# Storing the last chunk of a fused attention and gated-FFN kernel tile by tile, each tile copied out of PSUM by two engines in halves

## The chip, the cores and the metric

The kernel runs on 1 core of one Trainium2 chip. The metric is the device time of one launch in microseconds (us); lower is better. Beside it the hardware profiler gives one profiled launch of each kernel, whose span (first to last instruction) is some 2 us shorter than the time of a launch.

## The reference

Two stages. The first is attention over channels (B = 4, N = 6016 rows, C = 256 channels), the second a gated feed-forward network over the 24,064 rows that come out.

```python
def _attn_ref(q, k, v, tau):
    qn = q / (np.linalg.norm(q, axis=1, keepdims=True) + 1e-06)
    kn = k / (np.linalg.norm(k, axis=1, keepdims=True) + 1e-06)
    s = kn.transpose(0, 2, 1) @ qn / tau
    s = s - s.max(-1, keepdims=True)
    a = np.exp(s)
    a /= a.sum(-1, keepdims=True) + 1e-09
    return (v @ a).astype(np.float32)

def _moe_ref(x, w_gate, w_val, w_out):
    gate = 1.0 / (1.0 + np.exp(-(x @ w_gate)))
    val = x @ w_val
    return (gate * val @ w_out).astype(np.float32)
```

The inputs are fp32 random numbers, the output is fp32 of shape 24064 x 256.

## The kernel before

The rows of a batch are worked in 12 chunks: 11 of four 128-row tiles and a last one of three, since 6016/128 = 47. For each chunk the kernel computes gate and value products (`glu`) and, one chunk later, the output product of the chunk before (`out_mms`). An output tile of 128 x 256 fp32 collects in PSUM (the memory in which matmuls add up) over 12 matmuls, is copied to SBUF (from which the transfer takes it), and when the chunk's last tile is there, one transfer stores all of them.

```python
def out_mms(b, ci, n0, n1):
    t0, nt = groups[ci]
    hT = hts[b, ci]
    for n in range(n0, min(n1, nt * FC)):
        s, f = divmod(n, FC)
        if n == 0:
            ffn[b, ci] = opool.tile([P, TPC, C], FP32, tag="osb", name="out_sb")
        if f == 0:
            ffn["ps"] = pso.tile([P, C], FP32, tag="o", name="ps_o")
        mm(ffn["ps"], hT[:, f, ds(s * P, P)], w_out_sb[:, f, :], f == 0, f == FC - 1)
        if f == FC - 1:
            pending.append((ffn[b, ci], s, ffn["ps"], b, ci))

def flush():
    while pending:
        out_sb, s, ps, b, ci = pending.pop(0)
        t0, nt = groups[ci]
        nc.vector.tensor_copy(out=out_sb[:, s, :], in_=ps)
        if s == nt - 1:
            nc.sync.dma_start(out=out_rows[b][:, t0 : t0 + nt, :], in_=out_sb[:, :nt, :])

# ... the main loop; after it, the last chunk has only its output product left:
for s in range(groups[NCH - 1][1]):
    out_mms(*prev, s * FC, (s + 1) * FC)
    flush()
```

The framework in which it is written gives every transfer that SyncE or ScalarE issues one of eight completion semaphores (counters that tell when a transfer has landed), in turn, and puts closing waits for all of them at the end of SyncE's program.

Of the kernel before, what the change touches and what calls it, by code (L numbers as in the profile page):

```python
# [17 lines left out]
def kernel(  # L18
# [20 lines left out]
    nc = tc.nc  # L39
# [5 lines left out]
    B, N, C = q.shape  # L45
# [9 lines left out]
    NCH = (NT + TPC - 1) // TPC  # L55
# [8 lines left out]
    out_rows = out.rearrange("(b p t) c -> b p t c", b=B, p=P)  # L64
# [45 lines left out]
    t0, nt = groups0[0]  # L110
# [24 lines left out]
    for fg in range(NFG):  # L135
        for w, src in enumerate((moe_w_gate, moe_w_val)):
            nc.gpsimd.dma_start(
                out=w_sb[w][fg],
                in_=src.rearrange("(t p) f -> p t f", p=P)[:, :, ds(fg * FG, FG)],
# [290 lines left out]
    def flush():  # L430
        while pending:
            out_sb, s, ps, b, ci = pending.pop(0)
            t0, nt = groups[ci]
            nc.vector.tensor_copy(out=out_sb[:, s, :], in_=ps)  # L434
            if s == nt - 1:
                nc.sync.dma_start(out=out_rows[b][:, t0 : t0 + nt, :], in_=out_sb[:, :nt, :])


    def busy(n):
# [101 lines left out]
    for b in range(B):  # L541
        side = side_work(b)
        for ci in range(NCH):
            block = b + 1 < B and ci in (9, 10)
            for f in range(FC):
                glu(b, ci, f)
                flush()
                if prev is not None and not block:
                    out_mms(*prev, f * TPC, (f + 1) * TPC)
                for fn, a in side.get((ci, f), ()):  # L550
                    fn(*a)
                if (b, ci) == (0, 0) and f < len(gh_order) - 5:
                    gh(0, 5 + f, pso, "o")
            if prev is not None and block:
                for s in range(TPC):
                    for fn, a in side.get((ci, FC + s), ()):
                        fn(*a)
                    out_mms(*prev, s * FC, (s + 1) * FC)
                    flush()
            prev = (b, ci)  # L560
# [3 lines that stand above are left out]
# [35 lines left out]
```

## Time and profile before

| | before |
|---|---|
| time, median of 6 launches (3 of them taken before the change was run) | 832.36 us (832.06 to 832.71) |
| span of the profiled launch | 830.4 us |
| TensorE busy | 99% of the span |
| start of the last sigmoid (`g_sb`) | 822.03 us |
| from there to the end of the span, the **tail** | 8.39 us |

The last sigmoid serves as a mark: nothing before it is touched by the change, and everything that is touched lies after it. The tail is taken from the records at full resolution (the span ends at 830.415), so it may differ by 0.01 from what the rounded lines give. The lines of this profile stand in the prediction below.

### The profile page before, as it was taken

To read this page: it belongs to the slowest core of one execution; us is meant where nothing else is said; L and a number is where in the kernel's file an instruction comes from. 1 tells how busy PE (TensorE), PEld (TensorE's weight loads), DVE (VectorE), ACT (ScalarE), POOL (GpSimd) and SP (SyncE) were. 2 spreads that over 40 slices of the span, in tenths; PEclk is the share of its full clock that TensorE was granted. 3 is DMA by queue.
4 is the path that set the end of the run, shared out by engine and by line. 5 is a ranking of instruction groups with operands and counts; after the bars stand their busy time and mean duration, and the time that the engine had idled before them with its cause. 6 is when DMAs were issued, how large, how long until landed. Compare 5 with 4: busy or idle time off the path is not lost.

```text
span 830.4 us, 14273 instructions
## 1 busy us (share of the span) xinstructions
PE 818.9 (99%) x5463; PEld 513.8 (62%) x5474; DVE 570.4 (69%) x981; ACT 390.8 (47%) x642; POOL 82.9 (10%) x159
## 2 busy tenths in 40 slices
PE   8899999999999999999999999999999999999998
PEld 7656666666666666665576666666566566666666
DVE  2477777777667777777767777777766666666664
ACT  4554444445644444444654444444555444444442
POOL 5532100002110100000220020000000000000000
PEclk9999999999999999999999999999999999999999
DMA  9999623236755543233974453223222324323211
GB/s 209 207 206 189 130 52 88 51 63 123 141 105 105 102 105 60 56 52 79 161 140 97 84 112 77 51 75 66 62 56 65 75 51 82 71 49 69 47 36 71
DMA packets 78740, 77.21 MB, mean 93 GB/s; under 512 B 50768, under 2 KB 55632, under 8 KB 78672
## 3 DMA queue, kind: packets, MB, share of 16 engines
q0 software_dynamic: 23920, 38.81, 28.2%
q1 hardware_dynamic: 54608, 36.97, 17.4%
q8 instruction: 43, 0.70, 0.3%
q10 hardware_dynamic: 144, 0.52, 0.2%
q14 instruction: 25, 0.20, 0.1%
HBM read 78.64 MB, written 24.64 MB: 124 GB/s over the span
## 4 chain that ended last, share of the span: by engine, by line
PE 95%; DMA 3%; DVE 1%; issue 0%; POOL 0%; ACT 0%; POOLq 0%; DVEq 0%; ACTq 0%
PE ps_o L88 30%; PE ps_gate L88 29%; PE ps_val L88 29%; PE ps_s L88 4%; DMA k_sb<-in_k_dram 3%; PE ps_gh L88 2%; PE ps_n L88 0%; DVE gh_G L363 0%; PE ps_busy L88 0%; POOL q_sb L97 0%; PE ps_r L88 0%; DVE hT L408 0%; PE ps_rk L88 0%; DVE gh_H L363 0%; DVE x_sb L293 0%
## 5 line engine op out<-in xcount | busy, mean ns | idle before, releaser
L408 DVE TENSOR_TENSOR hT<-ps_val,g_sb 128x512 bf16<-128x512 f32 (+1 forms) x576 | 391.4, 680 | 214.7 <-ACT g_sb L407 209.5
L407 ACT ACTIVATE g_sb<-ps_gate 128x512 bf16<-128x512 f32 (+1 forms) x576 | 338.2, 588 | 386.6 <-PE ps_gate L88 379.0
L88 PE MATMUL ps_gate<-vT,gh_G 128*128 128x512 bf16 (+1 forms) x1152 | 337.6, 375 | 0.6 <-ACT g_sb L407 0.4
L88 PE MATMUL ps_val<-vT,gh_H 128*128 128x512 bf16 (+1 forms) x1152 | 337.7, 375 | 0.2
L88 PE MATMUL ps_o<-w_out_sb,hT 128*128 128x256 bf16 x2256 | 326.2, 273 | 0.0
L88 PEld LDWEIGHTS <-hT 128*128 128x128 bf16 x2256 | 220.7, 98 | 124.7
L88 PEld LDWEIGHTS <-gh_H 128*128 128x128 bf16 x1152 | 112.7, 98 | 131.5 <-DVE gh_H L363 0.5
L88 PEld LDWEIGHTS <-gh_G 128*128 128x128 bf16 x1152 | 112.5, 98 | 37.9 <-issue 0.6
L106 POOL DMA_DIRECT2D v_sb<-in_v_dram x48 | 25.6, 533 | 625.6 <-DMA vT<-v_sb 517.4
L434 DVE COPY out_sb<-ps_o 128x256 f32<-128x256 f32 x188 | 77.8, 414 | 13.5 <-PE ps_o L88 13.5
L88 PE MATMUL ps_s<-k_sb,q_sb 128*128 128x256 bf16 x376 | 66.8, 275 | 4.9 <-DMA k_sb<-in_k_dram 3.2
L212 DVE TENSOR_TENSOR acc<-acc,sq 128x1024 bf16<-128x1024 bf16 (+1 forms) x66 | 44.2, 670 | 0.0
L88 PEld LDWEIGHTS <-q_sb 128*128 128x128 bf16 x376 | 36.8, 98 | 11.1 <-issue 4.5
L173 DVE TENSOR_TENSOR sq<-q_sb 128x1024 bf16<-128x1024 bf16 (+2 forms) x45 | 30.0, 669 | 18.5 <-DMA q_sb<-in_q_dram 10.7
L97 POOL DMA_DIRECT2D q_sb<-in_q_dram x48 | 26.3, 548 | 15.6 <-DMA q_sb<-in_q_dram 7.9
L97 POOL DMA_DIRECT2D k_sb<-in_k_dram x48 | 26.4, 550 | 12.0 <-ACT g_sb L407 5.4
L173 DVE TENSOR_TENSOR sq<-k_sb 128x1024 bf16<-128x1024 bf16 (+2 forms) x34 | 22.4, 658 | 1.1 <-PE ps_n L88 1.1
L361 ACT ACTIVATE gh_G<-ps_gh,rrow 128x512 bf16<-128x512 f32 x22 | 15.1, 687 | 12.9 <-PE ps_gh L88 9.1
L171 ACT ACTIVATE sq<-k_sb 128x1024 bf16<-128x1024 bf16 (+1 forms) x12 | 12.1, 1020 | 14.7 <-DMA k_sb<-in_k_dram 13.2
L363 DVE TENSOR_SCALAR gh_H<-ps_gh,rrow 128x512 bf16<-128x512 f32 x23 | 17.1, 743 | 1.6 <-PE ps_gh L88 1.6
L88 PE MATMUL ps_busy<-ones_bf 128*128 128x128 bf16 x182 | 16.6, 244 | 1.1 <-DVE shift L125 1.1
L88 PEld LDWEIGHTS <-ones_bf 128*128 128x128 bf16 x194 | 14.6, 110 | 1.5 <-DVE shift L125 1.1
(54 smaller groups left out, 112.6 us busy)
## 6 DMA issues: line engine op xcount, KB each, us to landing
out_dram<-out_sb SPq DMA_DIRECT2D x44, 512.0 KB, 2.9
v_sb<-in_v_dram POOLq DMA_DIRECT2D x44, 256.0 KB, 3.9
q_sb<-in_q_dram POOLq DMA_DIRECT2D x43, 256.0 KB, 7.1
k_sb<-in_k_dram POOLq DMA_DIRECT2D x43, 256.0 KB, 8.3
out_dram<-out_sb SPq DMA_DIRECT2D x4, 384.0 KB, 2.5
w_gate<-in_moe_w_gate_dram POOLq DMA_DIRECT2D x3, 256.0 KB, 6.8
w_val<-in_moe_w_val_dram POOLq DMA_DIRECT2D x3, 256.0 KB, 6.8
w_out_sb<-in_moe_w_out_dram POOLq DMA_DIRECT2D x1, 768.0 KB, 11.9
```

The source lines that it names most:

```text
L88: nc.tensor.matmul(out, lhsT=lhsT, rhs=rhs, start=start, stop=stop, **kw)
L97: nc.gpsimd.dma_start(out=tl[:, :nt, :], in_=rows(src, b)[:, t0 : t0 + nt, :])
L106: nc.gpsimd.dma_start(out=v_sb[:, :nt, :], in_=rows(v, b)[:, t0 : t0 + nt, :])
L171: nc.scalar.activation(out=sq[:, :nt, :], in_=src[:, :nt, :], func=ACT.Square)
L173: engine.tensor_tensor(out=sq[:, :nt, :], in0=src[:, :nt, :], in1=src[:, :nt, :], op=ALU.mult)
L212: nc.vector.tensor_tensor(out=acc[:, :nt, :], in0=acc[:, :nt, :], in1=st[b]["sq", w][:, :nt, :], op=ALU.add)
L361: nc.scalar.activation(out=dst, in_=ps, func=ACT.Copy, scale=r)
L363: nc.vector.tensor_scalar(out=dst, in0=ps, scalar1=r, scalar2=None, op0=ALU.mult)
L407: nc.scalar.activation(out=g_sb[:, :n], in_=ps_gate[:, :n], func=ACT.Sigmoid)
L408: nc.vector.tensor_tensor(out=hts[b, ci][:, f, :n], in0=ps_val[:, :n], in1=g_sb[:, :n], op=ALU.mult)
L434: nc.vector.tensor_copy(out=out_sb[:, s, :], in_=ps)
```

## The change

The intent is to shorten the end. The last chunk's three tiles go out as they are ready, each in its own store, so that only a third of the bytes is left when the last matmul is over; and each tile's copy is shared by VectorE and ScalarE.

```diff
-            nc.vector.tensor_copy(out=out_sb[:, s, :], in_=ps)
-            if s == nt - 1:
-                nc.sync.dma_start(out=out_rows[b][:, t0 : t0 + nt, :], in_=out_sb[:, :nt, :])
+            if (b, ci) != (B - 1, NCH - 1):
+                nc.vector.tensor_copy(out=out_sb[:, s, :], in_=ps)
+                if s == nt - 1:
+                    nc.sync.dma_start(out=out_rows[b][:, t0 : t0 + nt, :], in_=out_sb[:, :nt, :])
+                continue
+
+            half = C // 2
+            nc.vector.tensor_copy(out=out_sb[:, s, :half], in_=ps[:, :half])
+            nc.scalar.copy(out_sb[:, s, half:], ps[:, half:])
+            nc.sync.dma_start(out=out_rows[b][:, t0 + s, :], in_=out_sb[:, s, :])
```

## The prediction

> **What bounds the kernel now.** I read the page first, then the timeline of the last eight microseconds, then the issues and packets of the last store, then the one place where this kernel already splits a copy between two engines.
>
> ```profile
> span 830.4 us, 14273 instructions
> PE 818.9 (99%) x5463; PEld 513.8 (62%) x5474; DVE 570.4 (69%) x981; ACT 390.8 (47%) x642; POOL 82.9 (10%) x159
> PE 95%; DMA 3%; DVE 1%; issue 0%; POOL 0%; ACT 0%; POOLq 0%; DVEq 0%; ACTq 0%
> L434 DVE COPY out_sb<-ps_o 128x256 f32<-128x256 f32 x188 | 77.8, 414 | 13.5 <-PE ps_o L88 13.5
> ```
>
> TensorE is busy 99% of the span and is 95% of the chain that ended last. The change touches no matmul, so whatever it does must happen after the last matmul, or by delaying one. The row of L434 gives the price of the operation that is cut in two: 414 ns for 128x256 fp32 out of PSUM. Only 3 of these 188 copies, those of the last chunk (3 tiles, because 47 tiles leave a last group of three), are changed. The timeline of the end, start and duration first:
>
> ```profile
> 822.15 4.53 PE L88 MATMUL ps_o<-w_out_sb,hT 128*128 128x256 bf16 x40
> 823.47 4.04 SPq L436 DMA_DIRECT2D out_dram<-out_sb  x2
> 824.10 0.42 DVE L434 COPY out_sb<-ps_o 128x256 f32<-128x256 f32 x1 [0.66 <-PE ps_o L88]
> 825.41 0.42 DVE L434 COPY out_sb<-ps_o 128x256 f32<-128x256 f32 x1 [0.88 <-PE ps_o L88]
> 826.72 0.42 DVE L434 COPY out_sb<-ps_o 128x256 f32<-128x256 f32 x1 [0.89 <-PE ps_o L88]
> ```
>
> The reader is to see that the three output tiles finish 1.31 us apart, that VectorE waits for each of them and that the first two copies have nothing behind them until the third is done: one store takes all three tiles. A timeline of 827.0 to 830.4 alone shows its issue at 827.17, 0.03 us after the last copy. From there to the end of the span are 3.2 us with no compute at all. Looking at DMA in that stretch (40 slices of 0.085 us):
>
> ```profile
> DMA  0200000000047997996999740000000000000000
> DMA packets 146, 0.40 MB, mean 117 GB/s; under 512 B 17, under 2 KB 17, under 8 KB 146
> q1 hardware_dynamic: 146, 0.40, 29.9%
> out_dram<-out_sb SPq DMA_DIRECT2D x1, 384.0 KB, 2.3
> SPq L594 <- DMA out_dram<-out_sb: 1.5, 1, 1.5
> ```
>
> The store needs some 0.8 us before its first packet, about 1.1 us of packets, and has landed 2.3 us after issue, at about 829.5; SyncE waits for that landing, and then the program's closing steps take 0.9 us. So the tail is: copy 0.42, gap 0.03, store 2.3, close 0.9. Only the copy and the packet part of the store can be changed by this diff.
>
> **What the Trainium skill says.** Perfetto Trace Analysis, section "Summary: the profiler window per engine type": the record of such a DMA instruction covers its issue and not the movement of data. The trace agrees: the chain of waits ends with the copy at 827.14 although the span runs to 830.4, so the chain alone would hide the part that the change aims at.
>
> PSUM — Partial Sum Buffer, section "PSUM bank collisions raise a hardware error": two engines may not access one bank on the same partitions at once, two reads included, even at different columns. Both halves of one output tile lie in one bank (256 fp32 a partition), so they must be ordered. The trace shows this ordering where the kernel already splits a copy (two rows of the timeline around 51 us):
>
> ```profile
> 51.42 0.41 DVE L382 COPY vT<-ps_tp 128x512 bf16<-128x512 bf16 x1
> 51.87 0.58 ACT L383 COPY vT<-ps_tp 128x512 bf16<-128x512 bf16 x1 [1.20 <-DVE vT L382]
> ```
>
> ScalarE had been idle for 1.20 us, its half was as ready as the other, and it began only 0.03 us after VectorE's half had ended. In the order of the changed kernel's instructions each new ScalarE copy likewise waits for VectorE, and each new store waits for ScalarE. So "in halves" means one after the other here.
>
> VectorE: DVE Perf Modes, section "The TRN2 errata — SBUF-src ops pay a fixed extra latency per instruction" gives for PSUM to SBUF 120 + N cycles at 0.96 GHz on VectorE and 172 + N at 1.2 GHz on ScalarE. For 256 fp32 on VectorE that is 392 ns against 414 measured, so the form holds: much of a copy is fixed, and half the columns don't take half the time.
>
> DMA: Bandwidth & Descriptors, section "Anatomy of one DMA — SWDGE (gpsimd) path" fits 2.0 us + bytes/436 GB/s. For 384 KB that is 2.9 us; measured are 2.3 on SyncE's queue, so the fixed part is smaller here, near 1.3 to 1.4, but the form (a large fixed part and a part by bytes) is the same.
>
> **The change part by part.** Nothing before the last chunk changes: the instructions of all five engines stand in the same order with the same waits up to there, on the order listing, so 822 us of the time are the same.
>
> *The copies of tiles 1 and 2* (done at 824.5 and 825.8 before) become two halves in a row, some 0.2 us later each, and each is followed by its own store. They lie beside matmuls: the third tile's first matmul (at about 825.4) needs tile 1's PSUM buffer back and now waits for ScalarE, but that half is over by about 824.7. No effect on the end. Their two stores of 128 KB go out at about 824.7 and 826.0; with 0.8 us to the first packet and 0.4 us of packets, the second is through by about 827.2, before the last store's packets, which start at about 828.1. SyncE is busy 0.34 us per issue in 1.31 us. No effect on the end either.
>
> *The last copy.* VectorE, 128 columns: 414 minus 128 columns' worth. In the table by form, the gate multiply takes 691 ns at 512 columns and 556 at 384, 135 per 128. So 414 - 135 = 279 ns. ScalarE, 128 columns: its sigmoid takes 597 ns at 512 and 487 at 384, 110 per 128; from the 585 ns copy above, 585 - 3 x 110 = 255 ns; from a 387 ns activation of 258 columns out of PSUM, 387 - 110 = 277. I take 265. The handover is the 0.035 us seen at 51.87. Together 0.28 + 0.035 + 0.265 = 0.58 against 0.42: **+0.16 us**, on the path.
>
> *The last store.* 128 KB in place of 384. In the stretch shown, queue 1 used 29.9% of 3.4 us, 1.02 us on each of the 16 engines, for 3 KB rows. The same view over 823.4 to 827.0 holds the chunk before with its 4 KB rows: 37.2% of 3.6 us, 1.34 us. So a further KB in each row costs 0.32 us, and an estimate for 1 KB rows is 1.02 - 2 x 0.32 = 0.38 us. The store should land 0.64 us sooner after its issue, 1.65 us instead of 2.3: **-0.64 us**, on the path. As a check, the page's median landings are 2.9 us at 512 KB and 2.5 at 384, 0.4 per 128 KB, which would give 0.8 less; but those medians fall among other traffic, so I keep 0.64.
>
> *Sum:* +0.16 - 0.64 = **-0.48 us**, of 832.23: **831.75 us**, 0.06% faster.
>
> **The rivals.** (a) *The halves run side by side.* Then the copy takes the longer half, 0.28, in place of 0.42, and the sum is -0.14 - 0.64 = -0.78: 831.45 us. Against it speaks the wait of 1.20 us shown above and the listing's waits. (b) *The landing is all fixed cost*, a small store takes as long as a large one, since most of it is the acknowledgement of the write. Then only the slower copy remains: 832.4 us. Against it: the packets take 1.1 of the 2.3 us in the view, and landing follows size in the medians. (c) *The extra stores get in the way*: the last store's packets queue behind tile 2's, or short rows run at a much lower rate than long ones, say at twice the time per byte, 0.7 us instead of 0.38. The gain shrinks to 0.1 or 0.2 us: 832.05. Against it: 0.9 us lie between tile 2's last packet and the last store's first. (d) *TensorE is held* at the third tile by the PSUM buffer that now comes free through ScalarE. That would need the copy to take 1.3 us instead of 0.58.
>
> **Range and chances.** The mechanisms span 831.45 to 832.4. The three times before spread over 832.15 to 832.71, so a median can shift by 0.2 without cause. I give 831.2 to 832.4. The whole tail after the last matmul is under 4 us, 0.5% of the time, so no outcome within it reaches 2% (16.6 us) either way: within 2% 0.99, the rest only for a disturbed run.
>
> **What would show each step right or wrong.** In the changed profile: three 128x128 copies on VectorE of about 0.28 us and three on ScalarE of about 0.265, each ScalarE one starting some 0.03 us after VectorE's end (if they overlap, rival a holds); the last issue about 0.6 us after the last matmul instead of 0.45; a landing of about 1.65 us for the last 128 KB (2.2 would be rival b, 1.9 to 2.0 rival c); a DMA view in which tile 2's packets are over before the last ones start; matmuls ending at the same 826.7; and a span near 829.9. The prediction is wrong if the span is not shorter, if TensorE shows a gap before the third tile, or if the program's close grows.

## The result

| | before | after |
|---|---|---|
| time, median of 6 launches | 832.36 us | 832.38 us |
| lowest to highest | 832.06 to 832.71 | 831.92 to 833.14 |
| span of the profiled launch | 830.4 us | 829.8 us |
| tail | 8.39 us | 8.29 us |

The ratio is 1.0001 with a 95% interval of 0.9988 to 1.0014: the same. Ratios are the mean time of one kernel's fast runs over that of the other's measured beside it, so not quite the ratio of the medians. The six runs of the changed kernel and the profiled run of the kernel before were at granted clocks of 0.998 to 1.0; the six times of the kernel before lie within 0.08% of each other.

The predicted 0.48 us is not there. What makes this worth reading is that the profiled span *is* shorter, by 0.6 us, about as predicted, and that nearly all of this is an accident. First the end of the timeline of the changed kernel (start, duration, engine, line, operation, in brackets the idle time before it and what ended it):

```profile
823.56 0.29 DVE L441 COPY out_sb<-ps_o 128x128 f32<-128x128 f32 x1 [0.66 <-PE ps_o L88]
823.88 0.27 ACT L442 COPY out_sb<-ps_o 128x128 f32<-128x128 f32 x1 [1.91 <-DVE out_sb L441]
824.17 2.95 SPq L443 DMA_DIRECT2D out_dram<-out_sb  x3
824.87 0.29 DVE L441 COPY out_sb<-ps_o 128x128 f32<-128x128 f32 x1 [1.02 <-PE ps_o L88]
825.20 0.27 ACT L442 COPY out_sb<-ps_o 128x128 f32<-128x128 f32 x1 [1.04 <-DVE out_sb L441]
826.18 0.29 DVE L441 COPY out_sb<-ps_o 128x128 f32<-128x128 f32 x1 [1.02 <-PE ps_o L88]
826.50 0.27 ACT L442 COPY out_sb<-ps_o 128x128 f32<-128x128 f32 x1 [1.04 <-DVE out_sb L441]
```

The halves run one after the other, as predicted: each ScalarE copy starts 0.03 us after VectorE's end. But the last copy begins at 826.18, and before it began at 826.72. That is 0.54 us *earlier*, although nothing ahead of it had been changed. The chain that ended last shows where the 0.54 us is from. Its lines (start, duration, link) around 32 us, of the kernel before:

```profile
21.80 10.48 DMA k_sb<-in_k_dram
32.33 1.03 PE ps_s L88 x8
```

and of the changed kernel:

```profile
22.00 9.75 DMA k_sb<-in_k_dram
31.79 1.03 PE ps_s L88 x8
```

The start of the kernel waits for loads of `k`. In this launch the last of these ended 0.54 us sooner, and comparing the matmuls of the two traces one by one, their difference stays at -0.54 us from there to the last matmul. Below, the kernel before run again arrives 0.81 us sooner than itself. So this part belongs to no kernel.

That leaves 0.09 us in the tail (8.387 against 8.293). The last store itself did what it should. The DMA view of the changed kernel from 826.4 to 829.8 (40 slices of 0.085 us):

```profile
DMA  9996200000000029998300000000000000000000
DMA packets 281, 0.25 MB, mean 75 GB/s; under 512 B 33, under 2 KB 281, under 8 KB 281
out_dram<-out_sb SPq DMA_DIRECT2D x1, 128.0 KB, 1.7
```

The first block is the second tile's store, over well before the last tile's store begins to move; that one needs some 0.5 us of packets where 384 KB needed 1.1, and lands 1.7 us after its issue where 2.3 were needed. The gain of 0.6 us on the store was made, the copy cost 0.17 us of it, and 0.37 us were lost after the landing. The view of SyncE's closing line, in the kernel before, first the stretch from 827.5 to 829.4, then from 829.4 to 829.6 (operation, count, shortest/median/longest ns, first and last start):

```profile
L594 SPq EVENT_SEMAPHORE  x8: 28/28/28, 827.5 to 828.0; - x8
...
L594 SPq EVENT_SEMAPHORE  x1: 27/27/27, 829.5 to 829.5; - x1
L594 SPq DRAIN  x1: 13/13/13, 829.6 to 829.6; - x1
```

and in the changed kernel, from 827.13 to 828.45 and from 828.45 to 828.96:

```profile
L601 SPq EVENT_SEMAPHORE  x2: 17/22/28, 827.2 to 827.5; - x2
...
L601 SPq EVENT_SEMAPHORE  x7: 28/28/28, 828.5 to 828.9; - x7
L601 SPq DRAIN  x1: 13/13/13, 828.9 to 828.9; - x1
```

These are nine closing waits, carried out strictly one after the other, at a pace of about 0.062 us. Before, eight of them were passed while the last store was still in flight, and only the ninth stood after the landing at 829.49. Afterwards only two were passed in flight; the third waits for the landing at 828.49, and six more follow it: 6 x 0.062 = 0.37 us. The built programs say why:

```
closing waits of SyncE, in order:   (first)  HW0  HW1  HW2  HW3  HW4  HW5  HW6  HW7
before: the last store signals on                                               HW7
after:  the three stores signal on           HW0  HW1                           HW7
        in the order HW7, HW0, HW1: the last one signals on HW1
```

One store became three, the turn of the eight semaphores moved on by two, and the last store's semaphore came to stand near the front of the row instead of at its end.

### The profile page after: what moved, and what is told of

Read it like the earlier page. It is cut to its first block, busy times and chain, and to the rows that moved or that the text cites. A ratio compares the mean times of both kernels' runs of the same rounds, so it can differ in the third digit from the quotient of the medians.

```text
span 829.8 us, 14281 instructions
## 1 busy us (share of the span) xinstructions
PE 817.7 (99%) x5463; PEld 512.9 (62%) x5474; DVE 569.7 (69%) x981; ACT 391.9 (47%) x645; POOL 83.2 (10%) x159
## 4 chain that ended last, share of the span: by engine, by line
PE 95%; DMA 3%; DVE 0%; issue 0%; POOL 0%; ACT 0%; POOLq 0%; DVEq 0%; ACTq 0%
PE ps_o L88 30%; PE ps_gate L88 29%; PE ps_val L88 29%; PE ps_s L88 4%; DMA k_sb<-in_k_dram 3%; PE ps_gh L88 2%; PE ps_n L88 0%; DVE gh_G L363 0%; PE ps_busy L88 0%; POOL q_sb L97 0%; PE ps_r L88 0%; DVE hT L408 0%; PE ps_rk L88 0%; DVE gh_H L363 0%; DVE x_sb L293 0%
```

## The experiments

The theory: three terms add up in the tail, namely the copy (+0.17 us for halves in a row), the store (-0.63) and the number of closing waits left after the last landing (0.062 us each). Rivals: the longer close comes from having several stores in flight, or from their late landing; or the halves are a gain after all; or the start's 0.54 us belongs to the change. All kernels gave correct results. Kernels looked at once carry the state "unknown", as a single run on one core does, and their times are not compared; what is compared is the tail, whose first part (last sigmoid to last copy) was 4.69 us in all of these profiles but that of the two-bank kernel. A further 0.02 to 0.03 us lie between the copy's end and the store's issue in every one. The terms, in us:

| kernel | last copy | issue to landing | landing to first closing drain | rest of close | tail |
|---|---|---|---|---|---|
| before | 0.42 | 2.32 | 0.08 | 0.84 | 8.39 |
| before, again | 0.42 | 2.31 | 0.08 | 0.84 | 8.38 |
| after | 0.59 | 1.69 | 0.45 | 0.84 | 8.29 |
| after, again | 0.59 | 1.70 | 0.45 | 0.84 | 8.30 |
| three stores, whole copies | 0.42 | 1.69 | 0.45 | 0.84 | 8.12 |
| one store, halves | 0.59 | 2.32 | 0.08 | 0.84 | 8.55 |
| before, one store cut early | 0.42 | 2.31 | 0.51 | 0.84 | 8.81 |
| before, four cut | 0.42 | 2.32 | 0.36 | 0.94 | 8.76 |
| before, five cut | 0.42 | 2.31 | 0.30 | 1.25 | 9.02 |
| after, six cut | 0.59 | 1.70 | 0.09 | 0.84 | 7.94 |
| three stores, whole copies, six cut | 0.42 | 1.70 | 0.08 | 0.84 | 7.77 |
| the same, again | 0.42 | 1.75 | 0.08 | 0.82 | 7.80 |
| two banks, six cut | 0.32 | 1.84 | 0.08 | 0.84 | 7.79 |

### The kernels run again

> The kernel before, unchanged, for the scatter. Theory: the tail repeats at 8.38 within 0.03, while the start of the last sigmoid (822.03 before, 821.49 after) moves by several tenths because the loads of the first 32 us end earlier or later. Rival, that the changed kernel's earlier arrival of 0.54 us belongs to the change: 822.03 again within 0.1.

> The changed kernel, unchanged, for the scatter: tail 8.29 within 0.03; the start of the last sigmoid anywhere from 821.4 to 822.7. Rival: 821.49 again within 0.1.

No edit. The tails repeat within 0.01 us. The last sigmoid of the kernel before started at 821.22, 0.81 us before its own first profile, and the span was 829.6, less than that of the changed kernel; the changed kernel's started at 821.38. So the rival falls: the 0.54 us at the start came with the launch and not with the change. The tails of these pairs agree to 0.01 us (a third pair below to 0.03), while a span is known only to about 1 us.

### Three stores, copies whole

```diff
             half = C // 2
-            nc.vector.tensor_copy(out=out_sb[:, s, :half], in_=ps[:, :half])
-            nc.scalar.copy(out_sb[:, s, half:], ps[:, half:])
+            nc.vector.tensor_copy(out=out_sb[:, s, :], in_=ps)
```

> Tail means: end of the span minus the start of the last sigmoid on ScalarE (before 830.4 - 822.03 = 8.38 us, after 829.8 - 821.49 = 8.29). This kernel keeps the three stores and gives each tile's copy back to VectorE whole. If the two halves run one after the other, as the trace says, the whole copy saves 0.29 + 0.03 + 0.27 - 0.42 = 0.17 us: tail 8.12. If the halves had in truth been a gain (side by side), the tail would be longer than 8.29, near 8.42.

The tail was 8.12 as expected. The second half of the change, two engines on one copy, is a loss of 0.17 us.

### One store, copies in halves

```diff
-            nc.sync.dma_start(out=out_rows[b][:, t0 + s, :], in_=out_sb[:, s, :])
+            if s == nt - 1:
+                nc.sync.dma_start(out=out_rows[b][:, t0 : t0 + nt, :], in_=out_sb[:, :nt, :])
```

> Halves kept, but one store of 384 KB for the whole chunk as before. Theory: only the copy's 0.17 us is added to the tail of before: 8.38 + 0.17 = 8.55, the landing is 2.3 us again and the closing row of waits is passed under the store's flight as before. Rival, that the halves cost nothing: 8.38.

The tail was 8.55, as expected. The same 0.17 us appear from the other side, and with one store the close is short again.

### The last store's place in the row of waits

To move the place and nothing else, stores far ahead of the end are cut in two. Each cut moves the turn of the semaphores on by one. In the kernel before, with one cut (n = 1):

```diff
+            if s == 1 and b == B - 1 and ci < 1:
+                nc.sync.dma_start(out=out_rows[b][:, t0 : t0 + 2, :], in_=out_sb[:, :2, :])
             if s == nt - 1:
-                nc.sync.dma_start(out=out_rows[b][:, t0 : t0 + nt, :], in_=out_sb[:, :nt, :])
+                r0 = 2 if b == B - 1 and ci < 1 else 0
+                nc.sync.dma_start(out=out_rows[b][:, t0 + r0 : t0 + nt, :], in_=out_sb[:, r0:nt, :])
```

> The kernel before with one much earlier store cut in two, so that all later transfers of SyncE and ScalarE use the next of the eight completion semaphores in turn, and the last store signals on the first of the eight that SyncE waits for at the close, not on the last one. The tail's own work is unchanged: one copy, one store of 384 KB. Theory of the position: 7 more waits at 0.062 us stand after the landing, tail 8.38 + 0.43 = 8.81, the closing steps after landing 1.35 us in place of 0.92. Rival, that the longer close comes from the number of stores in flight at the end or from their late landing: tail 8.38 unchanged.

The tail was 8.81, as expected, with the copy and the store unchanged. The same closing line of SyncE in this kernel, from 828.80 to 829.35; the store landed at 828.82:

```profile
L597 SPq EVENT_SEMAPHORE  x8: 27/28/28, 828.8 to 829.3; - x8
L597 SPq DRAIN  x1: 13/13/13, 829.3 to 829.3; - x1
```

The last store's own wait and the seven behind it all stand after the landing. There is one store at the end here and no late small one, so the rivals "several stores in flight" and "late landing" fall: a kernel whose tail does exactly the work of the kernel before became 0.42 us longer in its tail because a store 163 us ahead of the last one had been cut in two.

The counter-test is the same edit with `ci < 6` in the changed kernel, which puts its last store on the last semaphore:

> The changed kernel with six much earlier stores cut in two, so that its last store signals on the last of the eight semaphores of the closing row again. Theory of the position: the six waits after the landing go under the store's flight, 6 x 0.062 = 0.37 us less: tail 8.29 - 0.37 = 7.92, which is 0.46 below before, as the prediction had it (0.48). Rival (number of stores at the end): 8.29 unchanged.

The tail was 7.94 where 7.92 was expected. From 828.85 to 829.02, around the landing at 828.91:

```profile
L604 SPq EVENT_SEMAPHORE  x1: 28/28/28, 828.9 to 828.9; - x1
L604 SPq DRAIN  x1: 13/13/13, 829.0 to 829.0; - x1
```

Only the store's own wait is left after it, none behind that. With the place put right, the change gives 0.45 us, which is what had been predicted for it (0.48).

### Does the cost go by the number of waits?

The kernel before with four cuts (`ci < 4`) and with five (`ci < 5`):

> As the kernel before with four early stores cut in two: the last store signals on the fourth of the eight semaphores, so four waits stand after its landing. Theory of the position, if the cost goes by the number of waits: 4 x 0.062 = 0.25, tail 8.63. If being off the last place costs a fixed amount, it equals the run with one store cut, 8.81; if it is the number of stores, 8.38.

> The kernel before with five early stores cut in two: last store on the fifth of the eight semaphores, three waits after the landing: 3 x 0.062 = 0.19, tail 8.38 + 0.19 = 8.57. The run with four cut stores gave 8.76 where 8.63 was expected; 0.10 of that was one closing step of SyncE of 116 ns in place of 7. If that step belongs to cutting many stores, it shows here too (8.67); if it is an accident, 8.57.

The tails were 8.76 and 9.02 where 8.63 and 8.57 had been expected: missed, both. The term in question behaved: landing to first drain was 0.51, 0.36 and 0.30 us with seven, four and three waits left, against 0.08 with none, within 0.04 of 0.08 + 0.062 n. What missed is another step. SyncE's closing drains in the two kernels (from 828.3 to 829.9, and from 829.2 to the end):

```profile
L597 SPq DRAIN  x3: 7/13/116, 829.0 to 829.6; - x3
...
L597 SPq DRAIN  x3: 7/13/116, 829.6 to 830.3; - x3
```

One drain took 116 ns in place of 7; with four cuts it was the third, with five the second. It also began some 0.3 us late: 0.40 us after the step before it where other kernels have 0.09 us (third drain), and 0.37 us where they have 0.07 (second drain). Every cut puts two more instructions into SyncE's program (the transfer and a wait), and the slow step moved two instructions forward. In the kernels with six cuts and three stores, which have eight instructions more than that with four cuts, a gap of 0.37 to 0.38 us stands eight instructions further forward still, among the closing waits. No landing ended it: none came within 0.15 us ahead of its end, where a wait otherwise ends 0.02 us after the landing. There it lies under the flight of the last store and costs nothing.

So the slow step looks tied to a fixed place in SyncE's program, and the guess that it was an accident was wrong. Counted from the start of the trace, it is the 208th of SyncE's records in all six profiles that have so many; the other seven have 201 to 205 records and no such step. The traces hold one more sign. In each of the six, 0.65 to 0.76 us after the slow step begins, a packet of 8 KB starts on the queue that the profile calls `q14 instruction`; in the other seven that queue is still from 813 us until 1.5 us after the end of the span. This points to the loading of further instructions, but no run tests it, and the cause stays open.

### Everything put right, and its time

Whole copies, three stores, six cuts:

> Three stores, whole copies on VectorE, last store on the last semaphore of the closing row. Theory, if the three terms add up: tail 8.38 - 0.63 (store) = 7.75 us. In the time of whole runs that is 0.6 us or 0.08%, less than the scatter of 0.3 to 0.5 us between runs: within 2%, the interval may or may not leave out 1. If the terms don't add (the last landing hidden by another wait), the tail stays at 7.9 or above.

> The same kernel as e_whole_shift6, timed again for the time of whole runs: tail 7.77 again; theory: about 0.6 us below the kernel before in the mean, ratio near 0.9993, not clear of the scatter by five rounds alone. Rival, that the 0.6 of the first five rounds was the start's luck: medians equal within 0.1 us.

The tails were 7.77 and 7.80, so the terms add. In launches: median 831.43 against 832.02 us for the kernel before (5 and 9 runs), ratio 0.9991, interval 0.9978 to 1.0005; the second time 832.03 against 832.63, ratio 0.9992, interval 0.9980 to 1.0005. Both differences of the medians, 0.59 and 0.60 us, agree with the 0.61 us of the tails, and both intervals still hold 1. By launch times alone the gain is not shown; it is within 2% in any case.

### Two PSUM banks for the last tile

Why do the halves wait for each other? Two builds, without a launch, tell. With the ScalarE half written to an SBUF tile of its own its copy still waits for VectorE; with its half of the product in a second PSUM bank it waits for TensorE alone:

```
own SBUF tile:  TensorCopy hi_sb<-ps_o    128x128 [waits DVE]
own PSUM bank:  TensorCopy out_sb<-ps_hi  128x128 [waits PE]
```

So the shared SBUF tile is not the reason; it is what the halves share in PSUM, one tile and with it one bank, which these builds don't tell apart. The order is a wait in the built program. The second form was run, with six cuts:

```diff
-            mm(ffn["ps"], hT[:, f, ds(s * P, P)], w_out_sb[:, f, :], f == 0, f == FC - 1)
+                if (b, ci, s) == (B - 1, NCH - 1, nt - 1):
+                    ffn["hi"] = pss.tile([P, C // 2], FP32, tag="s", name="ps_hi")
+            if (b, ci, s) == (B - 1, NCH - 1, nt - 1):
+                for ps, c0 in ((ffn["ps"], 0), (ffn["hi"], C // 2)):
+                    mm(ps[:, : C // 2], hT[:, f, ds(s * P, P)],
+                       w_out_sb[:, f, c0 : c0 + C // 2], f == 0, f == FC - 1)
+            else:
+                mm(ffn["ps"], hT[:, f, ds(s * P, P)], w_out_sb[:, f, :], f == 0, f == FC - 1)
```

> The last tile alone is computed as two products of 128 columns in two PSUM banks, so that both engines may copy at once (its ScalarE copy then waits for TensorE and no longer for VectorE in the built program); tiles 1 and 2 copied in halves one after the other; last store on the last semaphore. The price: 24 matmuls of 128 columns for 12 of 256; twelve of TensorE's filler matmuls of 128 columns took 0.69 us before, 0.0575 each, so 24 take 1.38 in place of 1.31: +0.07. The copy takes 0.29 in place of 0.42: -0.13. Tail 7.77 (whole copy, same position) - 0.06 = 7.71. If separate banks don't let them run at once: 7.77 + 0.07 + 0.17 = 8.01. If the narrow matmuls run slower than the filler ones: above 7.77.

The two rows of the timeline that matter:

```profile
826.22 0.29 DVE L456 COPY out_sb<-ps_o 128x128 f32<-128x128 f32 x1 [0.99 <-PE ps_o L88]
826.27 0.27 ACT L458 COPY out_sb<-ps_hi 128x128 f32<-128x128 f32 x1 [0.75 <-PE ps_hi L88]
```

They overlap, and both halves are over in 0.32 us where 0.42 were needed for the whole. Still the tail was 7.79, not 7.71. The front part was 4.67 us, 0.02 less than elsewhere where 0.07 more had been expected; it is the landing that took 1.84 us after the issue in place of 1.70. Whether that belongs to the kernel is not settled (the whole-copy kernel's landing varied between 1.70 and 1.75). By its launches (831.95 against 832.63 us, ratio 0.9994, interval 0.9980 to 1.0008) it is no better than the simpler one.

## Why the prediction was wrong, point by point

- **"Nothing before the last chunk changes"**: right for the program. What the working lacked is how far a launch scatters there: the last sigmoid started anywhere from 821.17 to 822.16 us in 13 profiles. The expected span "near 829.9" came out at 829.8 by this scatter, which would have passed for a confirmation had the tails not been compared.
- **The copies of tiles 1 and 2 and their stores lie beside other work**: right. TensorE's front part of the tail was the same 4.69 us, and the second store's packets were through before the last one's.
- **The last copy, +0.16 us**: right, +0.17 (0.29 + 0.03 + 0.27 against 0.42), and right in its reason. Rival (a) falls.
- **The last store, -0.64 us**: right, -0.63 (1.69 against 2.32). Rivals (b) and (c) fall, and (d) with the equal front part.
- **"and then the program's closing steps take 0.9 us ... Only the copy and the packet part of the store can be changed by this diff"**: this is the step that failed. The close was taken as one fixed block. One of the views of the kernel before had listed eleven semaphore steps of SyncE there, the first at 827.5 while the store was still in flight, but they were not followed up. The close begins with a row of waits taken in a fixed order, of which as many are hidden as stand ahead of the last store's semaphore. The diff adds two transfers, and so it moved that store from the last place to the third of nine: +0.37 us. With this term the sum is +0.17 - 0.63 + 0.37 = -0.09 us, which is what the tails show (-0.09). The prediction's last sentence had named the close among what would make it wrong, but no rival followed it up and it had no share in the number.
- **Range and chances**: the range of 831.2 to 832.4 us held the median of 832.38 at its edge, and "within 2%" was right. But a change of 0.48 us was forecast that was not there; and by launch times of this scatter it could hardly have been seen.

On what the skill's pages said: the two readers of one bank were kept in order by a wait in the built program (0.59 us for both halves, against 0.32 us with two banks); what happens without that wait no run shows. The record of a transfer did end ahead of its data: the last store's record before the change lasts 0.33 us, and its packets start 0.8 us after issue. The fit of VectorE: DVE Perf Modes for copies out of PSUM was a little low (numbers below).

## What to carry to other kernels

At the end of a kernel, count what is left after the last transfer has landed, and look at the order of the closing waits: in this framework, splitting one store far ahead of the end moved the last one to another semaphore and the end by 0.42 us. Adding or removing a transfer of SyncE or ScalarE should do the same, though only splitting was run. As this framework builds it, two engines don't copy out of one PSUM bank at once. Two banks let them, but the tail was then no shorter than with the whole copy (7.79 against 7.77). Judge a change in a tail of 8 us by the tail, measured from a mark that the change can't move, and not by spans that scatter by twice the effect.

## What the Trainium skill lacked or had wrong

- No page has it: the close of a program, as this framework builds it, waits for each completion semaphore in turn, at about 0.062 us a wait, and only those ahead of the last transfer's own are hidden; landing to first drain took 0.08, 0.30, 0.36, 0.45 and 0.51 us with 0, 3, 4, 6 and 7 waits left.
- No page gives it a length: a stop of some 0.3 us (0.37 to 0.40 us from step to step) at the 208th of SyncE's records, in six profiles of six. Its cause is open; if it is the loading of instructions, it belongs to Runtime: NRT & Kernel Launch, section "Instruction fetch mechanics".
- DMA: Bandwidth & Descriptors, section "Anatomy of one DMA — SWDGE (gpsimd) path": its fit (2.0 us + bytes/436 GB/s) is for transfers from GpSimd, and the page has none for SyncE's. As an estimate from two stores here (rows of 1 KB and of 3 KB), 1.69 us for 128 KB and 2.32 for 384, the bytes go at 262,144 B / 0.63 us = 416 GB/s, close to the page, and the fixed part is 2.32 - 393,216 B / 416 GB/s = 1.37 us.
- VectorE: DVE Perf Modes, section "The TRN2 errata — SBUF-src ops pay a fixed extra latency per instruction": for 128 fp32 out of PSUM the estimate from its table is 258 ns on VectorE and 250 on ScalarE; measured were 292 and 266, and for 256 on VectorE 414 against an estimate of 392.
